# Second pair hashed head by head in four column groups; the first batch's plan and its load order rewritten

## The chip, the cores and the metric

The kernel runs on one core of a Trainium2 chip. The metric is the device time of one execution in microseconds (us): 339.31 as the median of three runs of the kernel before (339.14 to 339.33).

The engines have queues of their own and work side by side: TensorE (PE; PEld is its weight load), VectorE (DVE), ScalarE (ACT), GpSimd (POOL), and SyncE (SP), which here only issues DMAs. Sixteen DMA engines carry them out.

## The reference

Attention in which a query sees only keys of its own hash bucket, and behind it a gated feed-forward part. Shapes: 4 batches, 8 heads, 768 tokens, head size 64, 6 hash bits; model width 512, hidden width 1536.

```python
q_bits = einsum('bhsd,dk->bhsk', q, proj) > 0        # 6 bits; k_bits likewise
mask   = q_bucket[:, :, :, None] == k_bucket[:, :, None, :]
attn   = softmax(where(mask, q @ k.T / 8, -1e9))
x      = (attn @ v), heads side by side              # 3072 tokens x 512
ffn    = (gelu(x @ w_gate) * (x @ w_val)) @ w_out
out    = x + sigmoid(x @ w_res) * ffn
```

## The kernel before

**Stages.** The kernel takes one batch after the other. A batch is four pairs of heads, numbered 0 to 15 over the kernel; the first batch is pairs 0 to 3, "the first pair" to "the fourth pair" in the text. After a batch's attention comes its gate and value product (`gate_val`, L530), and its output projections (L562, L576) run inside the next batch's attention.

**A pair.** Its q, k and v are loaded (`load`, `load_v`) on SP's queue. `cast` writes q and k in bf16 into a tile `nat`. `tr` transposes the raw values in 32 by 32 blocks into `t32`, a matmul with the projection (`hash_mm`, L281) gives the bit sums in PSUM, `hash_tok` (L293) transposes them back to tokens, and `bits` (L302) writes the signs beside the cast values in `nat`, four operations for each side on the engines that the plan names. Then `nat` is transposed to `aug`, on TensorE with a copy behind it (`turn_pe` and `turned`, L378, L384, L386) or by a DMA transpose (`turn`, L364). The dot product of two `aug` columns holds score and bucket match in one.

**Chunks.** A pair has 9 chunks of 1024 scores: matmuls (`scores`, L505), one exponential on ScalarE (L516, 128x1024), and later the value matmuls (`values`, L480). Chunks 0 to 3 of a pair belong to its first head, chunk 4 to both heads, chunks 5 to 8 to the second. In the plan `('S', n)` is score chunk n of the first batch with its exponential, `('V', n)` its value matmuls. Two PSUM buffers hold scores, so S of n + 2 waits for the exponential of n. `vals_a` (a cast) and `vals_s` (three sums) make the value tile and its column sums on GpSimd. `finish` divides, and the first two pairs' result goes to `x_sb` by DMA transpose (L433).

**What sets the order.** For the first batch a plan written out by hand, `PLAN`, lists every step; the order of its entries is the order of the instructions in each engine's queue. All later batches follow tables and due slots that the change doesn't touch. Loads go into four rotating buffers for q, four for k and three for v: a load into a used buffer waits in SP's queue until the last reader of the old content is done, also when that reader stands later in the plan. Weights come in pieces by `load_w` on GpSimd's queue (`('w',)` in the plan; L245), converted to bf16 on the way.

Of the kernel before, what the change touches and what calls it, by code (L numbers as in the profile page):

```python
# [14 lines left out]


PLAN = [
    ('load', 1, 0), ('load', 1, 1), ('load_v', 0), ('load', 2, 0), ('load_v', 1), ('load', 2, 1),
    ('load', 3, 0), ('load_v', 2), ('load', 3, 1), ('proj', 's', 'pssp'), ('cast', 0, 1, 'p', 0, 6),
    ('proj', 'w', 'pppp'), ('cast', 0, 0, 'p', 6, 12), ('cast', 0, 0, 's', 0, 6), ('cast', 0, 1, 'p', 6, 12),  # L20
# [9 lines left out]
    ('vs', 0), ('load', 4, 0), ('load', 5, 1), ('load', 4, 1), ('load_v', 3),  # L30
    ('S', 2), ('turn', 0, 0, 6, 12, 'av'), ('tr', 1, 1), ('copy', 0, 0, 6, 12, 'v'),
    ('S', 3), ('turn', 0, 1, 6, 12, 'f'), ('hash', (1,), 2), ('hash', (1,), 3), ('hash', (1,), 0), ('hash', (1,), 1),
    ('copy', 0, 1, 6, 8, 's'), ('copy', 0, 1, 8, 12, 'v'), ('tokens', (1,)),
# [17 lines left out]
    ('S', 19), ('bits', 3, 0, 'vvvp'), ('turn_dma', 3, 0), ('vs', 2), ('turn', 2, 1, 6, 12, 'f'),  # L51
# [12 lines left out]
    ('S', 29), ('hash', (4, 5), 2), ('finish', 2, 0),  # L64
# [25 lines left out]
def kernel(  # L90
# [45 lines left out]
    hh_pool = ctx.enter_context(tc.tile_pool(name="hh", bufs=1))  # L136
# [11 lines left out]
    mm_ps = ctx.enter_context(tc.tile_pool(name="mm_ps", bufs=1, space=PSUM))  # L148
# [46 lines left out]
    projw = const.tile([P, 2, 32], FP32, name="projw")  # L195
# [17 lines left out]
    def spread(dst, engs):  # L213
        for a, eng in enumerate(engs):
            if eng is nc.scalar:
                nc.scalar.activation(dst(a), projn, AF.Copy)
            else:
                eng.tensor_copy(dst(a), projn)
# [20 lines left out]
    for s in range(3):  # L239
        n = KF // 3  # L240
# [8 lines left out]
    def nat_of(x):  # L249
        return nat[(2 * x[0] + x[1]) % NN]  # L250
# [13 lines left out]
    t32, hsum, htok = {}, {}, {}  # L264
# [8 lines left out]
    def hash_mm(jobs, dhs=(0, 1), hs_=(0, 1)):  # L273
        if jobs[0] not in hsum:
            hsum[jobs[0]] = mm_ps.tile([P, HT, 32], FP32, tag="r", name="hs")
        hs = hsum[jobs[0]]
        for hh in hs_:
            sl = slice(hh * T, hh * T + T)
            for dh in dhs:
                for j, x in enumerate(jobs):  # L280
                    nc.tensor.matmul(hs[32 * j:32 * j + 32, sl], projw[:, dh, :],  # L281
                                     t32[x][:, sl, dh, :], start=(dh == 0), stop=(dh == 1),
                                     tile_position=(0, 32 * j))

    def hash_tok(jobs, psum=False):
        n = 32 * len(jobs)
        if psum:
            ht = mm_ps.tile([P, HT, 32], FP32, tag="f", name="htp")
            nc.vector.transpose(ht[:n].rearrange("p c n -> p (c n)"),
                                hsum[jobs[0]][:n].rearrange("p c n -> p (c n)"))  # L290
        else:
            ht = hh_pool.tile([P, 3, HT // 3 + 1, 32], FP32, tag="ht", name="ht")[:, :, 0:HT // 3]
            nc.vector.transpose(ht[:n].rearrange("p a c n -> p a (c n)"),  # L293
                                hsum[jobs[0]][:n].rearrange("p (a c) n -> p a (c n)", a=3))
        for j, x in enumerate(jobs):
            htok[x] = (ht, j)
# [117 lines left out]
    av = {}  # L414
# [179 lines left out]
    ENG = {"v": nc.vector, "s": nc.scalar, "p": nc.gpsimd}  # L594
# [113 lines left out]
    def first_gv(i):  # L708
# [28 lines left out]
    for s in range(NSLOT, LAST):  # L737
        p, c = divmod(s, NCH)
# [60 lines left out]
```

## Time and profile before

| | |
|---|---|
| median of three runs | 339.31 us |
| the profiled execution | 338.95 us, span 337.2 us |
| granted TensorE clock | 0.998 |
| TensorE busy | 331.5 us (98%) |
| VectorE, ScalarE, GpSimd busy | 217.0, 213.3, 175.4 us |
| TensorE in the chain that ended last | 93% |
| first batch's attention, up to its gate and value product | 0 to 46.06 us |
| exponentials of the first batch | 36, the first at 8.33 us, the last ends at 45.38 us |
| bytes moved by DMA | 43.88 MB |

A busy TensorE is not yet TensorE at its peak: matmuls are pipelined, and their ends are modelled. In the timeline a row gives start, busy time, engine, line and operation, what it writes and reads, a count, and in brackets the idle time before it with what ended it. In the views of the DMA queues q1 is what SP issues, q0 what GpSimd issues.

### The profile page before, as it was taken

To read this page: it belongs to the slowest core of one execution; us is meant where nothing else is said; L and a number is where in the kernel's file an instruction comes from. 1 tells how busy PE (TensorE), PEld (TensorE's weight loads), DVE (VectorE), ACT (ScalarE), POOL (GpSimd) and SP (SyncE) were. 2 spreads that over 40 slices of the span, in tenths; PEclk is the share of its full clock that TensorE was granted. 3 is DMA by queue.
4 is the path that set the end of the run, shared out by engine and by line. 5 is a ranking of instruction groups with operands and counts; after the bars stand their busy time and mean duration, and the time that the engine had idled before them with its cause. 6 is when DMAs were issued, how large, how long until landed. Compare 5 with 4: busy or idle time off the path is not lost.

```text
span 337.2 us, 7848 instructions
## 1 busy us (share of the span) xinstructions
PE 331.5 (98%) x3138; PEld 202.7 (60%) x3138; DVE 217.0 (64%) x461; ACT 213.3 (63%) x246; POOL 175.4 (52%) x261
## 2 busy tenths in 40 slices
PE   7999999999999999999999999999999999999996
PEld 6667666565666655655666665666566665666444
DVE  7887675664577958875687896876567444343243
ACT  4889972237999962437999982255999984322220
POOL 5779930235389942575999972567977300000000
PEclk9999999999999999999999999999999999999999
DMA  7997999999866233616249923723150340000012
GB/s 231 373 286 132 222 237 182 187 159 232 287 204 177 62 95 78 107 36 98 92 108 272 303 77 92 135 49 62 35 124 33 80 103 31 33 0 0 33 62 94
DMA packets 74387, 43.88 MB, mean 130 GB/s; under 512 B 52544, under 2 KB 71360, under 8 KB 74352
## 3 DMA queue, kind: packets, MB, share of 16 engines
q1 hardware_dynamic: 67872, 37.95, 44.4%
q0 software_dynamic: 6400, 5.44, 10.5%
q8 instruction: 24, 0.39, 0.5%
q14 instruction: 11, 0.09, 0.1%
q10 hardware_dynamic: 80, 0.00, 0.0%
HBM read 29.56 MB, written 6.29 MB: 106 GB/s over the span
## 4 chain that ended last, share of the span: by engine, by line
PE 93%; ACT 3%; DVE 2%; issue 1%; DVEq 0%; ACTq 0%
PE sp L530 37%; PE fps L576 18%; PE sp L505 17%; PE av L480 9%; PE rps L562 6%; PE hs L281 3%; ACT ering L516 3%; PE wps L226 1%; ACT e L516 1%; PE hs L319 1%; PE pt L378 1%; PE pt L464 0%; DVE nat L329 0%; DVE o L582 0%; DVE aug L386 0%
## 5 line engine op out<-in xcount | busy, mean ns | idle before, releaser
L516 ACT ACTIVATE e<-sp 128x1024 bf16<-128x1024 f32 x117 | 117.7, 1028 | 8.3 <-PE sp L505 3.2
L339 POOL TENSOR_TENSOR pr<-ld,projr 128x384 f32<-128x384 f32 x96 | 93.8, 998 | 48.2 <-DVE sums L345 29.0
L547 ACT ACTIVATE gt<-sp 128x768 bf16<-128x768 f32 x48 | 38.9, 810 | 83.5 <-PE sp L530 77.9
L505 PE MATMUL sp<-aug,aug 71*128 71x256 bf16 (+1 forms) x384 | 86.2, 326 | 0.4
L576 PE MATMUL fps<-wo,hh 128*128 128x512 bf16 (+2 forms) x312 | 79.6, 363 | 0.0
L550 DVE TENSOR_TENSOR hh<-gt,sp 128x768 bf16<-128x768 bf16 x48 | 45.8, 954 | 44.2 <-PE sp L530 40.8
L530 PE MATMUL sp<-x_sb,wv 128*128 128x512 bf16 (+1 forms) x384 | 70.9, 326 | 0.0
L530 PE MATMUL sp<-x_sb,wg 128*128 128x512 bf16 (+1 forms) x384 | 70.9, 326 | 0.0
L480 PEld LDWEIGHTS <-e 128*128 128x128 bf16 x936 | 43.5, 97 | 25.9
L345 DVE TENSOR_REDUCE sums<-pr 128x6 f32<-128x384 f32 x96 | 50.0, 541 | 11.6 <-POOL pr L339 11.0
L530 PEld LDWEIGHTS <-wg 128*128 128x128 bf16 x384 | 37.0, 98 | 25.6 <-issue 1.2
L530 PEld LDWEIGHTS <-wv 128*128 128x128 bf16 x384 | 37.4, 98 | 25.0 <-issue 0.2
L480 PE MATMUL av<-va,e 128*128 128x65 bf16 x936 | 47.1, 193 | 0.0
L576 PEld LDWEIGHTS <-hh 128*128 128x128 bf16 x312 | 28.1, 97 | 22.0 <-issue 0.2
L505 PEld LDWEIGHTS <-aug 71*128 71x128 bf16 x384 | 29.0, 97 | 11.5 <-issue 2.0
L579 DVE SCALAR_TENSOR_TENSOR fps<-th,fps 128x512 f32<-128x512 f32 (+2 forms) x26 | 17.0, 652 | 26.2 <-PE fps L576 26.0
L516 ACT ACTIVATE ering<-sp 128x1024 bf16<-128x1024 f32 x27 | 25.9, 1031 | 3.0 <-PE sp L505 3.0
L562 PE MATMUL rps<-wr,x_sb 128*128 128x512 bf16 x96 | 27.1, 379 | 0.0
L566 ACT ACTIVATE th<-rps 128x512 f32<-128x512 f32 x24 | 14.3, 594 | 18.5 <-PE rps L562 18.5
L270 DVE STREAM_TRANSPOSE t<-ld 128x768 f32<-128x768 f32 (+3 forms) x28 | 22.9, 841 | 0.8 <-PE hs L281 0.6
L459 DVE COPY av<-av 128x390 f32<-128x390 f32 x24 | 13.5, 563 | 11.9 <-PE av L455 11.7
L260 POOL TENSOR_SCALAR nat<-ld 128x768 bf16<-128x768 f32 (+1 forms) x12 | 9.6, 804 | 17.7 <-DMA aug<-nat 16.8
(76 smaller groups left out, 256.2 us busy)
## 6 DMA issues: line engine op xcount, KB each, us to landing
ldv<-in_v_dram SPq DMA_DIRECT2D x16, 384.0 KB, 6.2
out_dram<-o SPq DMA_DIRECT2D x23, 256.0 KB, 2.0
ld<-in_q_dram SPq DMA_DIRECT2D x15, 384.0 KB, 5.7
ld<-in_k_dram SPq DMA_DIRECT2D x15, 384.0 KB, 5.6
wg<-in_moe_w_gate_dram POOLq DMA_DIRECT2D x4, 384.0 KB, 9.4
wv<-in_moe_w_val_dram POOLq DMA_DIRECT2D x4, 384.0 KB, 10.2
wo<-in_moe_w_out_dram POOLq DMA_DIRECT2D x3, 512.0 KB, 7.3
wr<-in_moe_w_res_dram POOLq DMA_DIRECT2D x1, 512.0 KB, 15.3
```

Source lines behind the costliest of these rows:

```text
L270: nc.vector.transpose(t32[p, side][:, sl].rearrange("p c h n -> p (c h n)"), raw[p, side][:, sl].rearrange("p c d -> p (c d)"))
L339: nc.gpsimd.tensor_mul(pr, raw[x][:, hi * T:(hi + 1) * T], projr[:, bit].unsqueeze(1).to_broadcast([P, T, D]))
L345: nc.vector.reduce_sum(sums[x][:, hi * T:(hi + 1) * T, bit], pr, axis=mybir.AxisListType.X)
L480: nc.tensor.matmul(av[p, hi][:, qt, :], e[:, off:off + P], va[:, hi, jt, 0:D + 1], start=first, stop=(repeats(p, hi) and jt == T - 1), ski ...
L505: nc.tensor.matmul(sp[:, off:off + nq * P], ks[0:KA, hi * T + jt, :], qs[0:KA, hi * T + qt0:hi * T + qt0 + nq, :], start=True, stop=True)
L516: nc.scalar.activation(e, sp, AF.Exp, scale=float(ALPHA))
L530: nc.tensor.matmul(sp[:, c0:c1], w[:, kk, bass.ts(m, P)], xs[:, kk, c0:c1], start=(kk == 0), stop=(kk == KM - 1))
L547: nc.scalar.activation(gt, sp[:, 0:S], AF.Gelu)
L550: nc.vector.tensor_mul(hidden[b][:, m, :], gt, ps[1][:, 0:S])
L562: nc.tensor.matmul(rps, x_sb[b][:, kk, t, :], wr[:, kk, :], start=(kk == 0), stop=(kk == KM - 1))
L576: nc.tensor.matmul(fps[:, cs], hh[:, m, bass.ts(t, P)], wo[:, m, cs], start=(m == 0), stop=(m == KF - 1))
L579: nc.vector.scalar_tensor_tensor(fps[:, cs], th[:, cs], 1.0, fps[:, cs], op0=ALU.add, op1=ALU.mult)
```

## The change

Only the first batch's code changes; every later instruction is as before, 26 lines further down in the file (L505 becomes L531, L516 becomes L542 and so on).

1. The second pair's hash is done by `hash_heads`: the four combinations of head and side (q or k) take a column group each, where before the two sides took a group each and the heads followed each other. The sums for 6 token columns of 128 partitions instead of 12 of 64 are turned by one transpose of three column blocks (`head_tokens`), and the bits are written head by head and side by side (`head_bits`): 16 operations on 6 token columns instead of 8 on 12.
2. `PLAN` is rewritten: nearly all steps of the first batch stand in another order, some on another engine.
3. The loads of the first batch are issued in another order.

```diff
+    def hash_heads(p, dh):
+        if dh == 0:
+            hsum[p] = ps_tile()
+        for g in range(4):
+            hi, side = divmod(g, 2)
+            nc.tensor.matmul(hsum[p][32 * g:32 * g + 32], projw[:, dh, :],
+                             t32[p, side][:, hi * T:(hi + 1) * T, dh, :], start=(dh == 0), stop=(dh == 1),
+                             tile_position=(0, 32 * g))
+
+    def ps_tile():
+        return mm_ps.tile([P, T, 32], FP32, tag="r", name="hs")
+
+    def head_tokens(p):
+        ht = hh_pool.tile([P, 3, HT // 3 + 1, 32], FP32, tag="ht", name="ht")[:, :, 0:T // 3]
+        nc.vector.transpose(ht.rearrange("p a c n -> p a (c n)"),
+                            hsum[p].rearrange("p (a c) n -> p a (c n)", a=3))
+        htok[p] = ht
+
+    def head_bits(p, side, hi, engs):
+        for a in range(4):
+            g = 32 * (2 * hi + side)
+            engs[a % len(engs)].tensor_scalar(
+                nat_of((p, side))[32 * a:32 * a + 32, hi * T:(hi + 1) * T, D:D + NBITS],
+                htok[p][g:g + 32, ..., NBITS * a:NBITS * (a + 1)], 0.0, 0.5,
+                op0=ALU.is_gt, op1=ALU.subtract)
...
-        hash1=hash_runs,
+        hash1=hash_runs, hash4=hash_heads, tokens4=head_tokens,
+        bitsh=lambda p, side, hi, e: head_bits(p, side, hi, [ENG[x] for x in e]),
...
-    ('S', 3), ('turn', 0, 1, 6, 12, 'f'), ('hash', (1,), 2), ('hash', (1,), 3), ('hash', (1,), 0), ('hash', (1,), 1),
+    ('S', 5), ('cast', 1, 1, 'p'), ('hash4', 1, 0), ('hash4', 1, 1), ('tr', 2, 0), ('V', 2), ('tokens4', 1),
```

Three places of the new order follow. In the rows, `ld0` is a load of q, `ld1` of k, `ldv` of v, and what stands behind `waits` are the counters that an instruction waits for: `DMAHW` is an earlier DMA, the others are engines.

SP's queue, first batch, before: from the fifth pair's loads on.

```order
L158 DMA ld0_285<-in_q_dram 128x2x384 [waits DVE_49,DMAHW6_49,Activation_49,Pool_49]
L158 DMA ld0_329<-in_q_dram 128x2x384 [waits DMAHW7_49,DVE_49,Pool_49]
L158 DMA ld1_331<-in_k_dram 128x2x384 [waits DMAHW0_49]
L158 DMA ld1_333<-in_k_dram 128x2x384 [waits DMAHW1_49,DVE_49,Pool_49]
L166 DMA ldv_335<-in_v_dram 128x2x384 [waits DMAHW2_49,Pool_49]
L166 DMA ldv_492<-in_v_dram 128x2x384 [waits DMAHW3_49,Pool_49]
L158 DMA ld1_617<-in_k_dram 128x2x384 [waits DMAHW4_49,DVE_49,Pool_49]
L433 DMA_TRANSPOSE x_sb_585<-x_tok_584 128x6x128 [waits DMAHW5_49,DVE_49]
L364 DMA_TRANSPOSE aug0_716<-nat2_133 128x12x128 [waits DMAHW6_49,DVE_49,Pool_49]
L364 DMA_TRANSPOSE aug1_744<-nat3_136 128x12x128 [waits DMAHW7_49]
L158 DMA ld0_746<-in_q_dram 128x2x384 [waits DMAHW0_49]
```

The same stretch of SP's queue now.

```order
L158 DMA ld0_287<-in_q_dram 128x2x384 [waits DVE_49,DMAHW6_49,Activation_49,Pool_49]
L158 DMA ld0_289<-in_q_dram 128x2x384 [waits DMAHW7_49,DVE_49,Pool_49]
L158 DMA ld0_291<-in_q_dram 128x2x384 [waits DMAHW0_49,DVE_49,Pool_49]
L166 DMA ldv_293<-in_v_dram 128x2x384 [waits DMAHW1_49]
L158 DMA ld1_358<-in_k_dram 128x2x384 [waits DMAHW2_49]
L158 DMA ld1_476<-in_k_dram 128x2x384 [waits DMAHW3_49]
L166 DMA ldv_546<-in_v_dram 128x2x384 [waits DMAHW4_49,Pool_49]
L158 DMA ld1_549<-in_k_dram 128x2x384 [waits DMAHW5_49,DVE_49]
L158 DMA ld1_551<-in_k_dram 128x2x384 [waits DMAHW6_49,DVE_49]
L459 DMA_TRANSPOSE x_sb_578<-x_tok_577 128x6x128 [waits DMAHW7_49,DVE_49]
L390 DMA_TRANSPOSE aug0_723<-nat2_133 128x12x128 [waits DMAHW0_49,DVE_49,Pool_49]
L390 DMA_TRANSPOSE aug1_750<-nat3_136 128x12x128 [waits DMAHW1_49]
```

Behind the two q loads for the fifth and sixth pairs stood k loads; now the seventh pair's q load stands there (third row), and its wait on GpSimd is for the cast of the third pair's q, whose buffer it takes over. Behind it stand a v load, two k loads, another v load and two more k loads, and behind these the transposes (last three rows) that make `x_sb` of the first pair and `aug` of the fourth pair.

GpSimd's queue, before: from the second pair's column sums to the cast of the third pair's q (last row).

```order
L399 TENSOR_TENSOR v3_420<-ldv_153 128x384
L401 TENSOR_TENSOR v1_422<-v3_420 128x128
L402 TENSOR_TENSOR vsum_419<-v1_422,v3_420 128x2x64
L403 MEMSET vsum_419 128x2
L245 DMA wg_141<-in_moe_w_gate_dram 128x4x384
L391 CAST va_478<-ldv_159 128x12x64
L392 MEMSET va_478 128x12
L391 CAST va_488<-ldv_153 128x12x64
L392 MEMSET va_488 128x12
L260 TENSOR_SCALAR nat2_133<-ld0_157 128x12x64
L262 CAST nat1_130<-ld1_155 128x12x64
L260 TENSOR_SCALAR nat0_127<-ld0_151 128x12x64
```

GpSimd's queue now, from the cast of the second pair's k to the first weight load.

```order
L262 CAST nat3_136<-ld1_187 128x12x64
L306 TENSOR_SCALAR nat2_133<-ht_410 32x6x6
L306 TENSOR_SCALAR nat3_136<-ht_410 32x6x6 x5
L306 TENSOR_SCALAR nat2_133<-ht_410 32x6x6 x2
L262 CAST nat1_130<-ld1_262 128x12x64
L417 CAST va_503<-ldv_282 128x12x64
L418 MEMSET va_503 128x12
L417 CAST va_506<-ldv_241 128x12x64
L418 MEMSET va_506 128x12
L260 TENSOR_SCALAR nat0_127<-ld0_191 128x12x64
L262 CAST nat3_136<-ld1_270 128x12x64
L245 DMA wg_141<-in_moe_w_gate_dram 128x4x384
```

The cast of the third pair's q (`nat0_127<-ld0_191`) now stands behind eight bits operations of the second pair, a k cast and the casts of two v tiles; the weight load that stood ahead of the v casts now follows it.

VectorE's queue, before: from the bits of the first pair's second key head to the second pair's first `aug` copy.

```order
L329 TENSOR_SCALAR nat1_130<-hs1_298 64x6x6 x2
L270 STREAM_TRANSPOSE t32_349<-ld1_147 128x768
L386 COPY aug0_262<-pt_342 71x768
L386 COPY aug1_257<-pt_356 71x512
L293 STREAM_TRANSPOSE ht_374<-hs_363 64x3x128
L302 TENSOR_SCALAR nat2_133<-ht_374 32x12x6 x4
L302 TENSOR_SCALAR nat3_136<-ht_374 32x12x6 x3
L386 COPY aug0_439<-pt_440 71x768
L270 STREAM_TRANSPOSE t32_471<-ld0_151 128x768
L386 COPY aug1_453<-pt_454 71x768
```

The same stretch now.

```order
L355 TENSOR_SCALAR nat1_130<-hs1_301 64x6x6 x2
L412 COPY aug0_244<-pt_339 71x768
L412 COPY aug1_237<-pt_351 71x768
L270 STREAM_TRANSPOSE t32_383<-ld1_187 128x768
L270 STREAM_TRANSPOSE t32_400<-ld0_191 128x768
L299 STREAM_TRANSPOSE ht_410<-hs_391 128x3x64
L306 TENSOR_SCALAR nat2_133<-ht_410 32x6x6 x3
L306 TENSOR_SCALAR nat3_136<-ht_410 32x6x6 x3
L306 TENSOR_SCALAR nat2_133<-ht_410 32x6x6 x2
L412 COPY aug0_433<-pt_434 71x768
L412 COPY aug1_445<-pt_446 71x768
```

The two copies that make the first pair's second heads stood behind the transpose of the second pair's k (`ld1_147`), and a part of the second copy was ScalarE's; now both stand ahead of it (`ld1_187`) and whole. The second pair's bits are eight half-size operations here and eight on GpSimd, where they were seven and one.

More of the change, by code (lines that the diff above doesn't have):

```diff
@@ L33 @@
-    ('copy', 0, 1, 6, 8, 's'), ('copy', 0, 1, 8, 12, 'v'), ('tokens', (1,)),
[8 rows of a table removed]
-    ('S', 12), ('hash', (2, 3), 2), ('hash', (2, 3), 3), ('copy', 1, 1, 6, 12, 'v'), ('cast', 2, 1, 'p'),
-    ('cast', 2, 0, 'p'), ('hash', (2, 3), 0), ('hash', (2, 3), 1), ('finish', 0, 0), ('tokens', (2, 3)),
-    ('bits', 2, 0, 'vvp'), ('bits', 2, 1, 'vp'),
[6 rows of a table removed]
-    ('S', 19), ('bits', 3, 0, 'vvvp'), ('turn_dma', 3, 0), ('vs', 2), ('turn', 2, 1, 6, 12, 'f'),
[12 rows of a table removed]
-    ('S', 29), ('hash', (4, 5), 2), ('finish', 2, 0),
[7 rows of a table removed]
-    ('preset', 4, 0), ('tokens', (4, 5)), ('repeat', 4, 0), ('gv', 1), ('cast', 4, 1, 'p'),
+    ('proj', 's', 'pssp'), ('tr', 0, 0, 0, 4), ('load', 1, 0), ('load_v', 0), ('fill', 32, 114), ('load', 1, 1),
[3 rows of a table added]
@@ new lines @@
+    ('turn', 0, 1, 0, 2, 'f'), ('load_v', 1), ('cast', 0, 0, 's', 0, 6), ('turn', 0, 0, 0, 4, 'r'),
+    ('cast', 0, 0, 'p', 6, 12), ('bits1', 0, 1, 2, 6), ('bits1', 0, 0, 4, 6), ('copy', 0, 1, 0, 2, 's'),
+    ('turn', 0, 1, 2, 6, 'f'), ('tr', 0, 0, 6, 12), ('load', 2, 1), ('copy', 0, 0, 0, 4, 's'),
+    ('turn', 0, 0, 4, 6, 'av'), ('copy', 0, 1, 2, 6, 'v'), ('copy', 0, 0, 4, 6, 's'), ('load', 3, 1),
+    ('cast', 0, 1, 'p', 6, 12),
+    ('S', 0), ('cast', 1, 0, 'p'), ('va', 0), ('load_v', 2), ('tr', 0, 1, 6, 12), ('tr', 1, 0), ('load', 5, 0),
@@ new lines @@
+    ('load', 4, 0), ('load', 6, 0), ('load_v', 3),
+    ('S', 1), ('hash1', 0, (0, 6, 12, 'av'), (1, 6, 12, 'av')), ('bits1', 0, 0, 6, 12), ('bits1', 0, 1, 6, 12),
+    ('vs', 0),
+    ('S', 2),
+    ('S', 3), ('turn', 0, 0, 6, 12, 'av'), ('copy', 0, 0, 6, 12, 'v'), ('proj', 'w', 'pppp'),
+    ('turn', 0, 1, 6, 12, 'f'), ('load', 5, 1), ('V', 0), ('V', 1), ('copy', 0, 1, 6, 12, 'v'),
+    ('S', 4), ('tr', 1, 1),
+    ('S', 5), ('cast', 1, 1, 'p'), ('hash4', 1, 0), ('hash4', 1, 1), ('tr', 2, 0), ('V', 2), ('tokens4', 1),
@@ new lines @@
+    ('S', 6), ('V', 3),
+    ('S', 7), ('bitsh', 1, 0, 0, 'vvvp'), ('turn', 1, 0, 0, 6, 'r'), ('bitsh', 1, 1, 0, 'pvvp'),
+    ('turn', 1, 1, 0, 6, 'f'), ('V', 4), ('bitsh', 1, 1, 1, 'ppvp'), ('bitsh', 1, 0, 1, 'pvpv'),
+    ('S', 8), ('load', 4, 1), ('V', 5), ('copy', 1, 0, 0, 6, 'v'), ('copy', 1, 1, 0, 6, 'v'), ('cast', 2, 1, 'p'),
+    ('tr', 3, 0),
+    ('S', 9), ('turn', 1, 1, 6, 12, 'f'), ('va', 2), ('va', 1), ('turn', 1, 0, 6, 12, 'r'),
+    ('S', 10), ('V', 6), ('V', 7), ('tr', 2, 1),
+    ('S', 11), ('load_v', 4), ('cast', 2, 0, 'p'), ('load', 6, 1), ('load', 7, 1), ('copy', 1, 1, 6, 12, 's'),
@@ new lines @@
+    ('tr', 3, 1), ('V', 8),
+    ('S', 12), ('cast', 3, 1, 'p'), ('copy', 1, 0, 6, 12, 'v'), ('hash', (2, 3), 2), ('finish', 0, 0),
+    ('hash', (2, 3), 3), ('hash', (2, 3), 0), ('hash', (2, 3), 1), ('w',),
+    ('S', 13),
+    ('S', 14), ('vs', 1), ('V', 9), ('V', 10), ('finish', 0, 1), ('V', 11), ('V', 12),
+    ('S', 15), ('tokens', (2, 3)), ('bits', 2, 1, 'vvvv'), ('turn', 2, 1, 0, 6, 'f'), ('bits', 2, 0, 'vvvp'),
+    ('S', 16), ('copy', 2, 1, 0, 6, 'v'), ('turn', 2, 0, 0, 6, 'r'), ('copy', 2, 0, 0, 6, 'v'),
@@ new lines @@
+    ('S', 17), ('turn', 2, 1, 6, 12, 'f'), ('tr', 5, 0), ('bits', 3, 1, 'pvvp'),
+    ('S', 18), ('bits', 3, 0, 'vvpp'), ('V', 13), ('cast', 3, 0, 'p'), ('turn_dma', 3, 0),
[15 rows of a table added]
+    ('S', 33), ('finish', 2, 1), ('load_v', 6), ('V', 31), ('finish', 3, 0), ('open', 4, 0),
+    ('S', 34), ('xturn', 2), ('V', 32),
+    ('S', 35), ('hash', (4, 5), 0), ('hash', (4, 5), 1), ('tr', 7, 1), ('cast', 5, 0, 'p'), ('V', 33), ('V', 34),
+    ('cast', 4, 0, 'p'), ('V', 35), ('finish', 3, 1), ('preset', 4, 0), ('tr', 7, 0), ('gv', 0), ('xturn', 3),
@@ L73 @@
+    ('tokens', (4, 5)), ('gelu',), ('gv', 1), ('repeat', 4, 0), ('va', 4),
 ]
```

5 lines of the change are left out of this document (removed), and 58 rows, old and new, of the table PLAN.

## The prediction

> **What bounds the kernel now.** First the chain of waits: its shares by engine, and the row in which the first batch hands over to its gate and value products.
>
> ```profile
> PE 93%; ACT 3%; DVE 2%; issue 1%; DVEq 0%; ACTq 0%
> ```
> ```profile
> 46.06 0.97 PE sp L530 x6
> ```
>
> From 46.06 us (L530 is the gate and value product) the chain runs on TensorE to the end, in code that the change leaves as it is. So the time moves by as much as this handover moves. What sets the handover is seen in ScalarE's timeline (start, busy us, line, operation, idle time before in brackets). E0 to E35 are the exponentials of the first batch's 36 score chunks, S0 to S35 their score matmuls.
>
> ```profile
> 8.33 1.94 ACT L516 ACTIVATE ering<-sp 128x1024 bf16<-128x1024 f32 x2 [0.50 <-PE sp L505]
> 10.45 2.00 ACT L516 ACTIVATE ering<-sp 128x1024 bf16<-128x1024 f32 x2 [0.18 <-PE sp L505]
> 12.35 0.37 ACT L384 ACTIVATE aug<-pt 71x256 bf16<-71x256 bf16 x1
> 14.06 4.84 ACT L516 ACTIVATE ering<-sp 128x1024 bf16<-128x1024 f32 x5 [1.34 <-PE sp L505]
> 18.95 3.89 ACT L516 ACTIVATE e<-sp 128x1024 bf16<-128x1024 f32 x4
> 23.78 8.62 ACT L516 ACTIVATE ering<-sp 128x1024 bf16<-128x1024 f32 x9 [0.95 <-PE sp L505]
> 32.30 3.77 ACT L516 ACTIVATE e<-sp 128x1024 bf16<-128x1024 f32 x4
> 35.91 8.52 ACT L516 ACTIVATE ering<-sp 128x1024 bf16<-128x1024 f32 x9
> 44.36 1.02 ACT L516 ACTIVATE e<-sp 128x1024 bf16<-128x1024 f32 x1
> ```
>
> The reader is to see two holes, 1.34 us (1.71 with the copy at 12.35) ahead of E4 and 0.95 ahead of E13, and from 23.78 on no hole at all: 23 exponentials up to 45.38, 0.94 us each. **Whatever holds one of these 23 back moves the end by as much.** E8 starts at about 17.93, E16 at 26.65, and E27, the first of the fourth pair, at 35.91 + 8.52/9 = 36.86.
>
> **The front: holes that shrink.** TensorE, from the chain and from its timeline:
>
> ```profile
> 11.73 1.75 PE hs L281 x16
> ...
> 21.70 1.44 PE hs L281 x32
> 23.14 0.56 PE sp L505 x3
> ```
> ```profile
> 11.23 0.50 PE L378 MATMUL pt<-ident,nat 128*71 128x128 bf16 x6
> ...
> 23.52 0.41 PE L480 MATMUL av<-va,e 128*128 128x65 bf16 x8
> ```
>
> The second pair's hash, two column groups wide, takes 1.75 us between S3 and S4. Four groups do 32 in 1.44, so the new 16 take 0.72: 1.03 us less of TensorE, and they now stand behind S5. A chunk's exponential starts 0.64 after its first score matmul (23.14 to 23.78). VectorE's rows:
>
> ```profile
> 10.23 0.39 DVE L325 STREAM_TRANSPOSE hs<-hs 128x192 f32<-128x192 f32 x1
> 10.66 0.40 DVE L329 TENSOR_SCALAR nat<-hs 64x36 bf16<-64x36 f32 x2
> ...
> 17.74 1.03 DVE L386 COPY aug<-pt 71x768 bf16<-71x768 bf16 x2
> 18.69 2.68 DVE L270 STREAM_TRANSPOSE t<-ld 128x768 f32<-128x768 f32 x3
> ```
>
> S4 needs the first pair's second heads. Their bits are ready at 11.06, as now; the key turn ends 0.50 later, the two copies, now both on VectorE and ahead of the transpose of the second pair's keys, at 12.37. S4 reads them then and E4 starts at 12.9 instead of 14.06: 1.16 us won.
>
> Part of it is lost at S8. The key transpose (2.68/3) ends at 13.25, the hash at 14.05, its token transpose (0.39) at 14.65. The second pair's bits are then 16 half-size operations, 8 of them on GpSimd, and S8 stands behind the turn of the keys' first head, which needs three of those 8. The trace shows none of this size. Its neighbours, in the next fence, are 12 columns wide (0.87 us for 4, 0.23 apart) and 72 (2.56 for 5, 0.53 apart); I take 0.35, on the line between them. The third ends at 15.85, the turn (0.50) near 16.35, the value matmuls ahead of S8 (0.41) at 16.75, and E8 starts at 17.4: 0.5 us earlier than now, 0.9 at the lower end, nothing at the upper one.
>
> The hole ahead of E13 is filled: the key copy for the second heads (0.37 us for 256 columns above, 0.8 for 768 as an estimate, the exponential's 1.0 as upper end) stands on ScalarE between E11 and E12, while TensorE does the third and fourth pairs' hash (1.44). E13 comes at 23.05 and, after another 0.2 hole ahead of E15, E16 at 26.05: **0.6 us won**, between 0 and 1. Everything up to S26 keeps that lead, and S27 could start at 35.45.
>
> **The loads: what takes it back.** The SP rows under "The change" show the order: the q load of the seventh pair now stands ahead of a v load, two k loads, another v load and two more k loads, and it reuses the third pair's q buffer. Its GpSimd wait is that pair's cast, which the new plan puts after S11. GpSimd's timeline:
>
> ```profile
> 4.36 0.87 POOL L218 COPY projw<-projn 32x12 f32<-32x12 f32 x4
> ...
> 8.66 0.82 POOL L262 CAST nat<-ld 128x768 bf16<-128x768 f32 x1 [0.18 <-DMA ld<-in_k_dram]
> 9.97 0.83 POOL L391 CAST va<-ldv 128x768 bf16<-128x768 f32 x1 [0.49 <-DMA ldv<-in_v_dram]
> ...
> 12.81 0.11 POOL L403 MEMSET vsum<- 128x2 bf16 x1
> ...
> 20.28 0.81 POOL L262 CAST nat<-ld 128x768 bf16<-128x768 f32 x1
> ...
> 24.02 2.56 POOL L302 TENSOR_SCALAR nat<-ht 32x72 bf16<-32x72 f32 x5 [2.13 <-DVE ht L293]
> ...
> 32.18 0.85 POOL L245 DMA_DIRECT2D wv<-in_moe_w_val_dram  x1
> ```
>
> A v cast with its sums takes 2.95 (9.97 to 12.92), the sums alone 2.13. The first v now lands where the k load did, at 8.66, so casts, sums, the moved projection copies (0.87) and the key cast end at 13.3, before the bits can start. Eight bits operations end at 17.55; the casts k, v, v and q in front of that load (0.82 each) at 20.85. Until then SP stands still, and seven loads follow at once. The moves on SP and the sixteen DMA engines:
>
> ```profile
> 26.37 1.30 SPq L433 DMA_TRANSPOSE x_sb<-x_tok  x1
> 28.04 3.17 SPq L364 DMA_TRANSPOSE aug<-nat  x2
> ```
> ```profile
> DMA to landing us min/median/max: 3.8/3.9/4.0
> ```
> ```profile
> 16.00:17.00 1.00, 1.00 (x18) 0.87 (x16) 0.72 (x2) 1.00 (x3) 0.92 (x4) 1.00 1.07 373
> 27.00:27.50 0.50, 0.50 (x12) 0.43 (x10) 0.47 (x2) 0.50 (x1) 0.46 (x1) 1.00 0.00 0
> 27.50:28.00 0.50, 0.50 (x16) 0.43 (x13) 0.45 (x3) 0.50 (x2) 0.45 (x1) 1.00 0.71 136
> 31.00:32.00 1.00, 1.00 (x15) 0.60 (x14) 1.00 (x3) 1.00 (x2) 0.84 (x3) 1.00 1.13 217
> ```
>
> The last two columns of the windows are the DMA engines' share and GB/s. Loads fill the engines at 373 GB/s, so one of 393 KB takes 1.05 us. The transposes that make the fourth pair's aug (393 KB each; the second row, landing 3.8 and 4.0 us after issue, so by 33.5) fill them at 217 GB/s: 1.85 us each, and the x_sb transpose, half as large, 1.0. They ran alone, after a pause with 0 GB/s; traffic began 1.2 us after the issue at 26.37. Weight loads come from GpSimd's queue (packets, MB, share of the 16 engines; first from 35 to 41 us, then from 32.18 to 35, then from 36 to 36.5):
>
> ```profile
> q0 software_dynamic: 525, 0.39, 44.4%
> ```
> ```profile
> q1 hardware_dynamic: 1044, 0.69, 93.3%
> ```
> ```profile
> q0 software_dynamic: 104, 0.08, 119.0%
> q1 hardware_dynamic: 13, 0.02, 11.7%
> ```
>
> One takes 44.4% of 6 us = 2.66 us of all engines, begins 2.8 us after its issue at 32.18 (no q0 row before 35), and holds SP's q1 down to 11.7% while it runs.
>
> The sum: traffic starts at 20.85 + 1.25 = 22.1; seven loads, 7.35; the first wg load, issued at 21.7 among them, 2.66; the x_sb transpose, 1.0; so 33.1. The two aug transposes, issued at 28 and 29.5 once the q cast is done on GpSimd, then need 3.7: 36.8. GpSimd has meanwhile gone on (sums 2.13, cast 0.82) and issues the first wv load at 31.0 (now 32.18), with traffic from 33.8, in the middle of them: + 2.66 = **39.4**. S27 waits for both, and every matmul behind it in TensorE's queue waits with it; E27 starts 0.64 later, at 40.05 instead of 36.86. The remaining nine exponentials follow at the same pace with no hole to give back, so the end moves by **+3.2 us**. The lead of 0.6 won in front is inside the wait and buys nothing.
>
> Against the profiled execution (338.95 us, span 337.2) that is 342.15; its median was 339.31, 0.36 more: **342.5**.
>
> Cost nothing: the x_sb copy put ahead of the gelu table load makes the first gelu 0.4 us late, under the fourth hash (1.44) that TensorE does meanwhile; if that cover went, 0.4. The weight loads queue behind the fifth pair's casts, of which one waits for the late transpose, and so are issued near 45.6 us, 6 us later than now; the second wg piece, 3 us after its issue plus 2.66, is there at 51, and the fourth product that reads it comes at about 59. GpSimd's half-size bits after the first three, and the v load that waits for the second pair's sums, stay inside the times above.
>
> **Rivals.** *The transposes don't wait for the loads.* If they overlap, or the backlog is 4 us smaller than counted, both land by 35.75, S27 doesn't wait and the front's 0.6 stands: 338.7 (338.3 at its best). It decides at one point, landing before 35.75. For it: shares above 1.0, so some work overlaps. Against it: loads alone already read 1.07. The Trainium skill's "DMA: Bandwidth & Descriptors", section "Where 436 GB/s comes from", has HBM bind loads and the fabric bind transposes inside SBUF, which would leave engines free for the transposes; the 1.07 beside 373 GB/s speaks against that here.
>
> *The weights let the transposes through.* If wv takes none or a third of its 2.66 us ahead of them, they land between 36.8 and 37.7, and the time is 339.9 to 340.8. Against it: 119% to 11.7% above, though the loser there was a load. The same page's "Queues, rings and completion order" says that each engine takes turns between queues, a whole packet at a time; by even turns this rival would be the case, by the row it would not.
>
> *Stragglers.* The x_sb transpose issued at 34.12 behind three loads and wv landed 8.2 us later:
>
> ```profile
> 34.12 1.31 SPq L433 DMA_TRANSPOSE x_sb<-x_tok  x1
> ```
> ```profile
> DMA to landing us min/median/max: 2.8/5.5/8.2
> ```
>
> Loads that start where the transposes end (33.4), 3 x 1.05 + 2.66 + 1.0, would give 40.2; it was 42.3. Two us more put the time at 344.6.
>
> **Chances.** Forecast (341.3 to 343.5) 0.52, weights let through 0.2, no wait 0.14, stragglers 0.14. The range leaves out most of the no-wait case and the far end of the last: 339.6 to 344.2. About 0.2% (0.7 us) is what a measurement here can tell from no change. Faster by more than that needs the no-wait case at its best: 0.06. Within: its rest and a part of the second rival, 0.14. Slower: 0.8.
>
> **What would show it.** E4 near 12.9, E8 near 17.4 and no hole of 0.95 ahead of E13: the front. SP idle until about 21 and then seven loads; 0 GB/s around 20: the wait on the cast. Aug transposes landing 10 us after issue, and one hole of some 3 us ahead of E27, whose releaser is the DMA: the loss. If that hole is absent, the sum of the engines' work is wrong; if E16 is later than 26.65, the bits are.

## The result, and the profile after

| | before | after |
|---|---|---|
| median (lowest to highest) of six executions | 339.28 us (339.14 to 340.94) | 355.34 us (348.57 to 357.19) |
| the profiled execution, its span | 338.95, 337.2 us | 355.69, 353.7 us |
| granted TensorE clock in it | 0.998 | 0.964 |
| granted clock of the six executions of after | | 0.964 to 0.985 |

The changed kernel is slower: ratio 1.0345, 95% interval 1.0269 to 1.0421. That ratio rests on the two least disturbed executions of after, 348.57 and 353.63 us, because the comparison leaves out those far above the fastest; in this kernel the lower clock that sets them apart is itself an effect of the change, as the experiments show. The direction and the place of the loss are as forecast, the size is not: 16 us where 3.2 were forecast.

ScalarE's timeline of the kernel after, in the columns of the prediction (L542 was L516):

```profile
12.56 1.94 ACT L542 ACTIVATE ering<-sp 128x1024 bf16<-128x1024 f32 x2 [0.57 <-PE sp L531]
...
17.08 1.02 ACT L542 ACTIVATE ering<-sp 128x1024 bf16<-128x1024 f32 x1 [0.46 <-PE sp L531]
...
22.68 8.48 ACT L542 ACTIVATE ering<-sp 128x1024 bf16<-128x1024 f32 x9 [0.24 <-PE sp L531]
...
34.68 1.07 ACT L542 ACTIVATE ering<-sp 128x1024 bf16<-128x1024 f32 x1
44.94 1.02 ACT L542 ACTIVATE ering<-sp 128x1024 bf16<-128x1024 f32 x1 [9.19 <-PE sp L531]
46.68 1.02 ACT L542 ACTIVATE ering<-sp 128x1024 bf16<-128x1024 f32 x1 [0.71 <-PE sp L531]
...
58.84 1.02 ACT L542 ACTIVATE e<-sp 128x1024 bf16<-128x1024 f32 x1 [0.91 <-PE sp L531]
```

E4 comes at 12.56 (forecast 12.9), E8 at 17.08 (17.4), E13 at 22.68 (23.05). E26 starts at 34.68; before it started at 35.91. Then comes one hole of 9.19 us, and E27 stands at 44.94 instead of 36.86. The second thing to see is behind it: the last nine exponentials come 1.74 us apart ((58.84 - 44.94) / 8), where they came 0.94 apart before, and each waits for TensorE.

Of the 16.74 us between the two profiled executions, these rows show 8.08 up to E27 and another 6.40 from there to E35 (58.84 against 44.36 is 14.48); the other 2.26 are lost behind E35.

SP's and GpSimd's timelines of after, and the answers on the landing of the x_sb transpose and of the two aug transposes:

```profile
8.98 12.32 SPq L158 DMA_DIRECT2D ld<-in_q_dram  x3
...
25.21 3.86 SPq L459 DMA_TRANSPOSE x_sb<-x_tok  x1
29.17 9.07 SPq L390 DMA_TRANSPOSE aug<-nat  x2
```
```profile
14.47 3.13 POOL L306 TENSOR_SCALAR nat<-ht 32x36 bf16<-32x36 f32 x8 [0.89 <-DVE ht L299]
...
20.08 0.82 POOL L260 TENSOR_SCALAR nat<-ld 128x768 bf16<-128x768 f32 x1
```
```profile
DMA to landing us min/median/max: 10.1/10.1/10.1
```
```profile
DMA to landing us min/median/max: 9.1/11.3/13.5
```

SP stands in its third q load until 21.3, until the cast that starts at 20.08 is done on GpSimd. The x_sb transpose, issued at 25.21, lands 10.1 us later (before: 2.8); the aug transposes take 13.5 and 9.1 us (before: 3.8 and 4.0). TensorE's list of waits and the windows of 2 us (busy time of PE, PEld, DVE, ACT, POOL, then granted clock, DMA share, GB/s; the fifth window is longer):

```profile
PE sp L531 <- DMA aug<-nat: 9.0, 1, 9.0
```
```profile
36.00:38.00 2.00, 0.00 (x0) 0.00 (x0) 0.99 (x2) 0.00 (x0) 0.00 (x0) 1.00 1.63 72
38.00:40.00 2.00, 0.00 (x0) 0.00 (x0) 0.00 (x0) 0.00 (x0) 0.00 (x0) 0.61 1.43 129
40.00:42.00 2.00, 0.00 (x0) 0.00 (x0) 0.00 (x0) 0.00 (x0) 0.00 (x0) 0.50 1.25 104
42.00:44.00 2.00, 0.19 (x1) 0.13 (x2) 0.00 (x0) 0.00 (x0) 0.18 (x1) 0.50 1.15 289
44.00:60.00 16.00, 16.00 (x136) 8.88 (x134) 2.18 (x6) 9.21 (x9) 10.96 (x17) 0.50 0.85 163
60.00:62.00 2.00, 2.00 (x31) 1.66 (x28) 0.99 (x2) 0.00 (x0) 0.00 (x0) 0.50 1.31 202
62.00:64.00 2.00, 1.95 (x16) 1.24 (x15) 1.63 (x4) 0.40 (x2) 0.00 (x0) 0.91 1.32 203
```

S27 waits 9.0 us for the aug transposes. While TensorE stands idle its granted clock falls to 0.50, and it stays there until 62 us, 18 us after TensorE has gone back to work without a pause. So the loss has two parts: a hole, and a TensorE at half speed behind it.

### The profile page after: what moved, and what is told of

The parts are those of the page before. It is cut to its first block, busy times and chain, and to the rows that moved or that the text cites. A ratio compares the mean times of both kernels' runs of the same rounds, so it can differ in the third digit from the quotient of the medians.

```text
span 353.7 us, 7809 instructions
## 1 busy us (share of the span) xinstructions
PE 336.2 (95%) x3091; PEld 206.0 (58%) x3138; DVE 217.0 (61%) x462; ACT 214.3 (61%) x246; POOL 177.1 (50%) x267
## 4 chain that ended last, share of the span: by engine, by line
PE 89%; DMA 5%; POOL 2%; issue 1%; DVE 1%; SPq 0%; ACT 0%; POOLq 0%; DVEq 0%
PE sp L556 35%; PE fps L602 17%; PE sp L531 17%; PE av L506 9%; PE rps L588 6%; DMA aug<-nat 3%; DMA ldv<-in_v_dram 2%; PE hs L281 2%; PE wps L226 1%; PE pt L404 1%; POOL v L425 1%; POOL nat L306 0%; PE hs L345 0%; POOL va L417 0%; PE pt L490 0%
## 5 line engine op out<-in xcount | busy, mean ns | idle before, releaser
L542 ACT ACTIVATE e<-sp 128x1024 bf16<-128x1024 f32 x117 | 117.7, 1028 | 9.1 <-PE sp L531 4.1
L531 PE MATMUL sp<-aug,aug 71*128 71x256 bf16 (+1 forms) x384 | 90.0, 338 | 9.3 <-DMA aug<-nat 9.0
L602 PE MATMUL fps<-wo,hh 128*128 128x512 bf16 (+2 forms) x287 | 74.5, 361 | 1.3
L556 PEld LDWEIGHTS <-wv 128*128 128x128 bf16 x384 | 37.5, 98 | 24.9 <-issue 0.2
L531 PEld LDWEIGHTS <-aug 71*128 71x128 bf16 x384 | 29.6, 99 | 22.1 <-DMA aug<-nat 9.1
L542 ACT ACTIVATE ering<-sp 128x1024 bf16<-128x1024 f32 x27 | 26.5, 1024 | 15.6 <-PE sp L531 15.5
L588 PE MATMUL rps<-wr,x_sb 128*128 128x512 bf16 x91 | 26.0, 379 | 0.2
L450 DVE RECIPROCAL rec<-av 128x6 f32<-128x6 f32 x32 | 6.0, 188 | 24.9 <-PE av L478 18.8
```

The lines of the kernel that those rows point to most:

```text
L531: nc.tensor.matmul(sp[:, off:off + nq * P], ks[0:KA, hi * T + jt, :], qs[0:KA, hi * T + qt0:hi * T + qt0 + nq, :], start=True, stop=True)
L542: nc.scalar.activation(e, sp, AF.Exp, scale=float(ALPHA))
L556: nc.tensor.matmul(sp[:, c0:c1], w[:, kk, bass.ts(m, P)], xs[:, kk, c0:c1], start=(kk == 0), stop=(kk == KM - 1))
L588: nc.tensor.matmul(rps, x_sb[b][:, kk, t, :], wr[:, kk, :], start=(kk == 0), stop=(kk == KM - 1))
L602: nc.tensor.matmul(fps[:, cs], hh[:, m, bass.ts(t, P)], wo[:, m, cs], start=(m == 0), stop=(m == KF - 1))
```

## The experiments

In what follows "the hole" is TensorE's idle time ahead of S27.

### The hole and the half clock apart

**keep_busy**, the changed kernel with work in the hole:

```diff
+    def keep(n):
+        f = mm_ps.tile([P, 512], FP32, tag="f", name="keep")
+        for _ in range(n):
+            nc.tensor.matmul(f, ones.to_broadcast([P, P]), ones.to_broadcast([P, 512]), start=True, stop=True)
...
+    ('keep', 34),
     ('S', 27), ('V', 24), ('V', 25),
```

> 34 matmuls of 512 columns, whose result nobody reads, stand ahead of S27 in TensorE's queue (about 7 us of the 9.0 us hole). Theory A, two losses: the wait itself (E27 at 44.94 against 36.86, so 8.1 us) and the half clock that follows the hole, 16.1 less 8.1 = 8.0 us. With the hole filled the clock stays at 1.00, S27 still waits to about 43.8, the last nine exponentials come 0.95 apart, and the time is about 347.4 us. Rival C: the half clock has another cause (the time, the work in the stage); then the row shows 0.50 again from 40 to 62 us and the time stays at 353 to 356. Rival D: the filler itself holds S27 back; then S27 starts later than 44 with the idle ahead of it at nothing.

Lowest 347.57 us, at a granted clock of 1.00; median 351.1. The page's clock row and ScalarE's rows of the 347.57 us execution:

```profile
PEclk9999999999999999999999999999999999999999
```
```profile
34.99 1.07 ACT L543 ACTIVATE ering<-sp 128x1024 bf16<-128x1024 f32 x1
44.73 7.56 ACT L543 ACTIVATE ering<-sp 128x1024 bf16<-128x1024 f32 x8 [8.67 <-PE sp L532]
52.22 1.02 ACT L543 ACTIVATE e<-sp 128x1024 bf16<-128x1024 f32 x1
```

S27 comes as late as ever (E27 at 44.73), but the clock stays up, the eight exponentials from E27 on take 7.56 us together, and the time is within 0.2 us of the 347.4 that the hole alone was expected to give. So the hole is worth 8.1 to 8.3 us here, and the other 8.1 us of the kernel after's profiled execution (355.69 against 347.57, with E27 0.2 us apart) are the half clock. Rival C falls: the work in that stage runs at full clock when no idle time precedes it. The other five executions were at 350.5 to 355.9 us, so that the medians are only 4.2 us apart (355.34 and 351.1). Three of these five have a mean granted clock of 0.998 to 1.00, and what made them longer is not shown; the section on the front gives one candidate.

### What makes the transposes late

**q7_late** moves the load that SP waits in; **q7_early** does that alone to the kernel before; **wv_late** takes the weight load from beside the transposes.

```diff
-    ('load', 4, 0), ('load', 6, 0), ('load_v', 3),
+    ('load', 4, 0), ('load_v', 3),
...
-    ('S', 20), ('turn_dma', 3, 1), ('V', 15),
+    ('S', 20), ('turn_dma', 3, 1), ('load', 6, 0), ('V', 15),
```

> Theory A, the load that waits: SP stands still until 21 us because the seventh pair's q load waits for the third pair's q cast, and everything lost follows from it. With that load behind the second aug transpose the other loads run from 9 us on, both aug transposes land before 36 us, TensorE's idle ahead of S27 is under 0.5 us, the granted clock stays at 1.00, E27 starts at about 35.7, and the front's lead of 1.2 us stands: 337.8 to 338.6 us, 0.997 of before. Theory B, the backlog without the wait: the v load of the fifth pair waits for the second pair's sums on GpSimd until 23.7 anyway, the weight load falls among the loads behind it, and S27 still waits 2 us or more: 341 or above.

348.11 us median (346.46 to 348.82), ratio 1.0244 (1.0193 to 1.0296). Theory B held. TensorE's waits and the windows, in an execution of 346.61 us:

```profile
PE sp L531 <- DMA aug<-nat: 2.6, 1, 2.6
```
```profile
36.00:38.00 2.00, 0.32 (x1) 0.13 (x2) 0.00 (x0) 0.05 (x1) 0.31 (x1) 0.73 1.28 256
38.00:40.00 2.00, 2.00 (x21) 1.49 (x20) 1.06 (x2) 1.02 (x1) 2.00 (x3) 0.50 1.11 363
...
50.00:52.00 2.00, 2.00 (x31) 1.27 (x32) 1.10 (x3) 1.40 (x3) 0.00 (x0) 0.86 1.32 199
```

The hole shrinks from 9.0 to 2.6 us, so moving this load is worth 6.4 of it: SP's wait, and with it the 1.05 us of the load's own traffic, which no longer stands ahead of the transposes. What is left is enough for the clock to fall, for 13 us this time.

q7_early, the kernel before with `('load', 6, 0)` moved from behind the second `turn_dma` to behind `('load', 4, 0)`:

> The kernel before with one step moved: the seventh pair's q load from behind the second aug transpose to behind the fifth pair's q load. Theory A: SP stands still until the third pair's q cast on GpSimd (about 22 us), six loads and three transposes follow, the transposes land at 39 to 42 instead of 33.5, S27 waits 3 to 6 us, and where the hole is longer than about 4 us the clock halves: 342 to 352 us. Rival B: the wait needs the rest of the new plan (the second k load, the weight load among the loads) to reach S27; then the time stays within 1 us of 339.3.

339.63 us, ratio 1.0009 (0.9974 to 1.0045): rival B held. SP waits until 20.3 there too, yet the aug transposes land soon after their issue and TensorE has no wait:

```profile
DMA to landing us min/median/max: 4.6/4.8/5.0
```

In the plan of before the second pair's column sums and the first wg load come earlier on GpSimd (wg at 16.39 us against 21.62), and the traffic is down to 66 GB/s from 29 to 30 us, where the kernel after still moves 358 GB/s from 31 to 32. The wait in SP's queue is necessary for the 9 us, not sufficient.

wv_late, with the second `('w',)` behind `('cast', 5, 1, 'p')`, which itself waits for the aug transposes:

> The changed kernel with the first wv piece issued behind a cast that itself waits for the aug transposes, so that no weight load runs beside them. Theory A, the weight load blocks them: the first aug transpose starts at 34.3 as now, the second follows at once, both are there by about 38.5, the hole ahead of S27 shrinks from 9.0 to about 4 us, E27 starts at about 39.7; 342.1 us if the clock stays at 1.00, up to 350 if it halves again. Rival E, the transposes are slow by themselves in this place (one begins only when the one before has landed): they still land at 41 or later, and the time stays above 350.

349.79 us (348.75 to 352.4). TensorE's row:

```profile
43.40 1.04 PE L531 MATMUL sp<-aug,aug 71*128 71x512 bf16 x2 [4.68 <-DMA aug<-nat]
```

Everything up to S26 is 3.9 us later in this execution (the section on the front says why), so the hole is what counts: 4.7 us, near theory A's "about 4". The weight load beside the transposes is worth 4.3 us of the hole. It overlaps with the 6.4 of the moved load, since both delay the same transposes. The clock halved here too, from 41 to 47 us.

**hold_no_weights** leaves the load order alone and puts both weight pieces behind that cast:

> The changed kernel with its load order as it is (SP stands still until 21 us), and both first weight pieces behind the cast that waits for the aug transposes. Theory A (work of the engines adds up): the seven loads end at about 29.5, the x_sb transpose at 31, the aug transposes at 35 to 36; hole ahead of S27 at most 1.5 us: 338 to 341 us, more only where the clock halves. Rival F (each transpose starts when the one before has landed, and the seven loads come first): landing at 38 or later, a hole of 3 us or more, and the half clock: 345 to 350.

348.95 us median (344.99 to 353.3), ratio 1.0191 (1.0149 to 1.0234). TensorE's row, and windows of 1 us:

```profile
37.52 0.60 PE L531 MATMUL sp<-aug,aug 71*128 71x512 bf16 x2 [2.88 <-DMA aug<-nat]
```
```profile
30.00:31.00 1.00, 0.86 (x12) 0.63 (x12) 1.00 (x2) 1.00 (x3) 0.26 (x2) 1.00 2.61 279
31.00:32.00 1.00, 1.00 (x21) 0.80 (x20) 0.97 (x4) 1.00 (x3) 0.92 (x2) 1.00 0.64 54
32.00:33.00 1.00, 1.00 (x24) 0.76 (x21) 1.00 (x3) 1.00 (x2) 0.82 (x3) 1.00 0.53 108
33.00:34.00 1.00, 1.00 (x16) 0.69 (x13) 0.94 (x2) 1.00 (x2) 0.00 (x0) 1.00 1.27 290
34.00:35.00 1.00, 0.65 (x11) 0.47 (x9) 0.97 (x3) 1.00 (x2) 0.00 (x0) 1.00 2.18 214
35.00:36.00 1.00, 0.00 (x0) 0.00 (x0) 0.50 (x1) 0.59 (x1) 0.00 (x0) 1.00 0.06 7
```

This run takes the prediction's sum apart. Without wg and wv its terms give 22.1 + 7.35 + 1.0 + 3.7 = 34.15; S27 starts at 37.52. The loads end near 30.5, a microsecond later than counted (29.45); behind them, where the sum has one transpose after the other at full rate, the last two columns show pauses: 54 and 108 GB/s from 31 to 33, 7 GB/s from 35 to 36. Rival F is nearer, in the hole (2.88) and in the time. Its mechanism, that one transpose starts only when the one before has landed, isn't shown: the trace doesn't mark which transfer a packet belongs to.

### The repair, and what else waits

**weights_late** is q7_late with both weight pieces behind the cast.

> q7_late with both first weight pieces issued behind the cast that waits for the aug transposes, so that the stretch from 24 to 36 us has three loads and three transposes and nothing else. Theory A (the engines' total work ahead of the transposes decides): 2.66 us of wg go away ahead of them and 2.66 of wv among them, so both land by about 34.5 instead of 37.5, the hole ahead of S27 is under 0.3 us, the clock stays at 1.00, the front's lead of about 1 us stands: 338.0 to 338.8 us. Rival F (a transpose in this place takes its 4 to 6 us whatever runs beside it, and its start is set by the q cast on GpSimd at 28.6): they land at 36 or later, a hole of 1 us or more remains, 340 or above.

339.96 us median (339.61 to 346.53). The hole ahead of S27 is gone, but TensorE's and VectorE's waits show the next one:

```profile
PE hs L281 <- DVE t L270: 1.5, 1, 1.5
```
```profile
DVE t L270 <- DMA ld<-in_q_dram: 3.1, 1, 3.1
```

Moving the q load behind the transposes made its own reader late: `('tr', 6, 0)` at S28 holds VectorE, the fifth pair's transpose stands behind it, and TensorE's hash waits for that. Eight of the twelve executions are at 339.6 to 340.1 us with a granted clock of 0.998 to 1.00, four at 344.6 to 346.5 with 0.98 to 0.99.

**loads_ahead** (the two k loads ahead of the v load) and **late_keep** (q7_late with ten matmuls in its hole):

> weights_late, and in it the k loads of the seventh and eighth pairs stand ahead of the v load that waits for the second pair's sums until about 23. Theory A: SP issues them at 19 to 22, at most one load is left when the x_sb transpose is issued, the aug transposes land by about 33, no hole ahead of S27, clock 1.00: 338.0 to 338.6 us, the same as weights_late or a little better, faster than both kernels. Rival F as there: 340 or above.

> q7_late (hole of 2.6 us ahead of S27, clock at 0.50 from 37 to 51 us) with 10 matmuls of 512 columns in the hole, about 2.1 us of work. Theory A, the hole alone costs E27 at 38.8 against 36.9, and the rest of its 7 to 9 us is the half clock: with the hole filled the clock stays at 1.00 and the time is about 341.3 us. Rival C, the half clock comes of something else: 346 to 349 as without the filler.

341.84 us (339.52 to 346.63) and 347.44 us (344.26 to 350.14). Both missed, and both have the same VectorE wait behind S27 (1.6 and 2.2 us on TensorE). loads_ahead shows what that short hole can cost. Its profiled execution, 343.46 us, has the half clock only behind the hole, from 41 to 48 us: its last six exponentials, from 40.70 to 48.57, take 3.2 us more than at 0.94 us each. Six of the twelve executions, at a granted clock of 1.00, took 339.5 to 340.3; another 0.8 us of the difference is a wait of TensorE at 13 us in that one execution. In late_keep the clock stays at 1.00 through the filled hole, up to 44 us, against rival C, and falls behind the second one. Its best execution, 344.26 us, is near what the two holes add up to; why its median is 3 us above that isn't shown.

The next three kernels move `('tr', 6, 0)` from S28 to S32.

> weights_late, with the seventh pair's q transpose on VectorE moved from behind S28 to behind S32. In weights_late VectorE stands 3.1 us at that transpose, because its load now lands at 39, and the fifth pair's q transpose queued behind it holds TensorE's hash (a hole of 1.5 us, and then the half clock in 5 of 12 executions). Theory A: with it moved no TensorE hole is left, the clock stays at 1.00 in all executions, the front's lead of about 1 us stands to the end: 338.0 to 338.6 us, 0.996 to 0.998 of before. Rival H: the lead is eaten elsewhere (the late weights, the chain's other waits): 339 to 340.

> loads_ahead with the same transpose moved. Theory A: 338.0 to 338.6 us as in weights_tr_late, no hole. Rival H: 339 to 340.

> q7_late with the same transpose moved, both weight pieces where the new plan has them. Theory A: only the hole of 2.6 us ahead of S27 is left, the clock halves after it, E27 comes at 38.8 as in q7_late: 345 to 348 us. If the second hole was what kept the clock down, 341 to 343.

q7_tr_late: 348.88 us (343.12 to 354.08), with a hole of 3.7 us ahead of S27 and the half clock behind it; theory A, so the second hole wasn't what kept the clock down. weights_tr_late and ahead_tr_late have no hole behind 10 us, and reach 338.05 and 338.39 us. But their medians are 340.97 and 339.54: in 9 of 12 and 6 of 12 executions the time was above 340. Windows of weights_tr_late, an execution of 340.81 us:

```profile
8.00:10.00 2.00, 1.97 (x37) 1.08 (x35) 1.62 (x3) 1.95 (x3) 1.39 (x3) 0.75 1.02 337
10.00:12.00 2.00, 2.00 (x16) 0.75 (x6) 1.28 (x5) 0.87 (x2) 1.76 (x7) 0.50 1.06 386
...
14.00:16.00 2.00, 2.00 (x17) 0.96 (x18) 1.82 (x3) 0.74 (x1) 0.00 (x0) 0.54 1.06 372
```

The clock halves here from 9 to 16 us, behind the first pair's hash, where TensorE has short holes that both plans share. Of the 15 executions above 340 us 12 have a mean clock of 0.99, as this one. The kernel before was above 340 us too, in 22 of its 98 executions beside these experiments, but 20 of these have a mean clock of 1.00, and none was traced.

One trace shows that the clock figure can miss a slow front. The first two rows are the same five score matmuls in the kernel after and in wv_late, the third is a window of wv_late:

```profile
9.41 1.21 PE L531 MATMUL sp<-aug,aug 71*128 71x512 bf16 x5
```
```profile
11.30 1.89 PE L531 MATMUL sp<-aug,aug 71*128 71x512 bf16 x5
10.00:12.00 2.00, 2.00 (x35) 0.86 (x29) 0.56 (x3) 1.03 (x2) 1.75 (x7) 1.00 1.07 386
```

From 8 to 16 us the 512-column matmuls of wv_late take 607 to 634 ns each, as in the half-clock stretch of weights_tr_late (623 to 631), where others take 380; yet the clock column reads 1.00, because this trace's record of the clock begins only at 16.8 us. So TensorE was slow through the whole front, and that is why everything up to S26 came late there. Whether the executions with a mean clock of 1.00 above 340 us had such a front is open.

**weights_front, ahead_front, before_front** are these two and the kernel before, with three matmuls in the first of those holes:

```diff
     ('hash1', 0, (0, 4, 6, 'w0'), (1, 2, 6, 'w1')),
+    ('keep', 3),
```

> weights_tr_late with three matmuls of 512 columns (0.64 us), whose result nobody reads, behind the first pair's hash, where TensorE waits for the first bits from about 5.3 to 6.1 us. Theory A (a hole can cost the clock wherever it lies): the executions with the half clock at 9 to 15 us become rare, nearly all are at 338.0 to 338.9 us, median 338.4, faster than before by 0.7 to 0.9. Rival I (the half clock at the front comes of the first 4 us, of how the chip stood before the start, or of something else): the same mixture of 338.1 to 338.9 and 340.2 to 343 as in weights_tr_late.

> ahead_tr_late with the same three matmuls. Theory A: nearly all executions at 338.2 to 338.9 us. Rival I: half of them at 340.2 to 342.

> The kernel before with the same three matmuls at the same place. Theory A: the executions above 340 us (8 of 23) become rare, the others stay at 338.7 to 339.3. Rival I: a third above 340 us as without them.

Above 340 us were 2 of 12, 5 of 12 and none of 12; without the matmuls it was 9 of 12, 6 of 12 and 22 of 98. By the mean clock, 12 of the 24 executions of the two changed kernels were at 0.99 without the matmuls and none with them (two of ahead_front at 0.995). That speaks for theory A, but with ahead_front's times hardly moved, and the two sets of runs taken on different chips, it is not settled. weights_front is the best version found: 338.57 us median against 339.21, ratio 0.9982 (0.9949 to 1.0016). Ten of its twelve executions lie at 337.9 to 339.0 us; that it beats the kernel before is not shown.

### The hash alone

**hash_alone** is the kernel before with `hash4`, `tokens4` and `bitsh` in the places of the second pair's `hash`, `tokens` and `bits`.

> The kernel before with the second pair's hash, token transpose and bits done head by head, on the same engines and in the same places, and nothing else of the change. TensorE saves 1.03 us between S3 and S4, the token transpose takes 0.38 instead of 0.57, VectorE's bits 14 of 0.20 instead of 7 of 0.23, so 1.2 us more. Theory A: the hole ahead of E4 shrinks by 0.9 to 1.0 us, a half of it or more is left at E27, no new wait: 338.3 to 339.0 us. Rival G: VectorE's longer bits take it back at S8, within 0.3 us of 339.2.

339.31 us, ratio 1.0009 (0.9988 to 1.0029): rival G. ScalarE's rows:

```profile
13.38 4.84 ACT L542 ACTIVATE ering<-sp 128x1024 bf16<-128x1024 f32 x5 [0.70 <-PE sp L531]
18.92 3.89 ACT L542 ACTIVATE e<-sp 128x1024 bf16<-128x1024 f32 x4 [0.70 <-PE sp L531]
```

E4 gains 0.68 us, and a new hole of 0.70 ahead of E9 takes it back; E9 starts where it did (18.95). Twice as many bits operations on VectorE (2.74 us instead of 1.62) hold back the copies behind them, and S9 waits 0.78 us for one; that costs what TensorE saves. So the hash alone doesn't bring the changed kernel's lead in front. The rest of the new order must have a part in it; which step isn't tested.

## Why the prediction was right about the sign and wrong about the size

- **The front: right.** Each point came within 0.4 us of its forecast, all on the early side; 0.29 of it is E0, which started at 8.04 instead of 8.33 in this execution. The bits that were estimated at 0.35 us apart are 0.39 apart. The lead is worth nothing behind the hole, as said. Of the repaired versions, weights_front's traced execution keeps 0.3 us of it to the end; ahead_front's has 0.68 at the first batch's last exponential and 0.03 left in the second batch, where TensorE waits for GpSimd at 110 us.
- **The wait in SP's queue: right,** to 0.1 us (the cast ends at 20.9, forecast 20.85). But q7_early shows that the argument leaned on it too much: in the old plan the wait alone costs nothing.
- **The sum of the loads and transposes: the first step that failed.** S27 was to start at 39.4; it started at 43.8. Of the 4.4 us, 3.4 remain with both weight pieces away (34.15 against 37.52): 1.0 in the loads, which end near 30.5 instead of 29.45, and 2.4 in the terms for the transposes. These were added as busy time of the DMA engines, from a place where they ran alone, and here pauses stand among them. The other 1.0 is the weights, 6.3 us for two pieces (43.8 less 37.5) instead of 5.3.
- **"The remaining nine exponentials follow at the same pace": the second step that failed,** and the larger one. It priced a hole at its length. The trace of before could not have shown otherwise, its mean clock being 0.998, but the step was written as a fact, without a bound. It cost 8.1 us in the profiled execution, by keep_busy's. With it falls the claim that the time moves by as much as the handover moves: the code behind it is unchanged, but TensorE was still at half clock up to 62 us, and 2.26 us were lost behind E35.
- **The rivals.** No wait, and weights that let the transposes through, were both wrong: wv beside the transposes cost 4.3 us of hole, more than its 2.66 of engine time. Stragglers were nearest (landing later than the sum), with 2 us of the 4.4. None had the clock.
- **Cost nothing: not contradicted in the first batch.** The repaired versions issue the first two weight pieces far later and have no TensorE wait on weights up to 64 us; the one wait there is 0.8 us of weights_front for the aug transposes ahead of S27. Behind that, ahead_front lost its lead: GpSimd got its copy of `pr` in at 86.18 us (82.12 before), after a longer wait for that DMA. Whether the late weights cause it isn't shown.

Even the forecast's own hole of 3.2 us would probably have given more than 342.5: the profiled executions of hold_no_weights and q7_tr_late have holes of 2.9 and 3.7 us, with the half clock behind them, and took 347.4 and 346.6.

## What to carry to other kernels

Price a new TensorE hole of a microsecond or more at its length and, as a second case, at its length plus 3 to 8 us for the half clock behind it; cheap matmuls in the hole tell the two apart in one run. A load that waits in an in-order queue is dangerous through what stands behind it and what joins it there: move the weight loads away from DMA transposes that something waits for, and then look for the readers of whatever was moved back. Don't add up DMA transposes by their engine time when they are queued behind a backlog.

## What the runs showed that was not expected

The granted clock falls after short holes. It fell in the hole of 9.0 us after some 3.6 us of idle time, in q7_late in a hole of 2.6 us, and in one execution of loads_ahead just behind one of 1.6 us; in six others of that kernel the mean clock stayed at 1.00. The Trainium skill's "TensorE: Matmul & The Clock Gate", Part 1, has the clock halve after an idle window of about 3.4 us that runs free of the program; the first case agrees, the other two holes are shorter than that.

It comes back late. TensorE was busy without a pause from 43.8 us in the kernel after, and the clock rose at 62; in q7_late it took 13 us of work, in wv_late 4. The same part of the page has it return after one busy window of about 3.4 us; only wv_late is near that. What sets the time isn't shown: in the kernel after it rose as the product's matmuls began (61.8 us), but in q7_late it rose ahead of the product.

One regularity stands in the traces' records of the clock. The stretches at half clock behind a hole last 3.41 us (late_keep), 6.83 (wv_late, loads_ahead), 10.24 (q7_tr_late), 13.65 (q7_late, hold_no_weights) and 23.89 us (the kernel after), all of them multiples of 3.41. So in these runs the clock is set for whole stretches of 3.41 us, and a hole that ends the full clock costs at least one. Why a short hole ends it in one execution and not in the next may then be a matter of where it falls between two such points; that isn't tested.
